# Chunk 0's triangular inverse: the step sizes move from its end into its start, and eight narrow products join TensorE's queue

## The chip, the cores and the metric

The kernel runs on one core of a Trainium2 chip. TensorE (PE) multiplies matrices, VectorE (DVE), ScalarE (ACT) and GpSimd (POOL) work on rows of SBUF and PSUM, and SyncE (SP) mostly issues DMAs. Each engine has a queue of its own and works through it in order; waits between engines are semaphores. The metric is the device time of one execution in microseconds; lower is better.

## The reference

The reference is a delta-rule attention followed by a feed-forward layer. For each of 4 x 8 heads, with 768 tokens of 48 values:

```python
k_n = k / (np.linalg.norm(k, axis=-1, keepdims=True) + 1e-06)
for t in range(S):
    y[:, :, t] = np.einsum('bhd,bhde->bhe', q[:, :, t], state)
    v_old = np.einsum('bhde,bhd->bhe', state, kt)
    state = state + bt[:, :, :, None] * np.einsum('bhd,bhe->bhde', kt, vt - v_old)
```

The heads' outputs, 3072 tokens of 384 values, then go through `h = x @ w_in`, `g = h * sigmoid(h)` and `g @ w_out` with 2048 inner values.

## The kernel before

**Chunks.** The 768 tokens of a head are cut into six chunks of 128. In a chunk the recurrence becomes a triangular system: with G the products of keys with keys, the kernel needs a matrix X that solves it, each row scaled by a step size that comes from beta and the key's length. The inverse is found on blocks of 32 tokens (T = 32), and four such blocks are then joined to 128 by small products on TensorE. Chunk 0 has a start of its own, because nothing else can be computed before it: there VectorE inverts halves of 16 (Q = 16), and TensorE joins 16 to 32, 32 to 64.

**The start, chunk 0, in order.**
- `square`, `add_squares`, `norm_steps`: lengths of the keys, by GpSimd and VectorE, and the step sizes, spread over the rows (`spread`).
- `turn(0, b, ...)` transposes keys and queries on TensorE (L500), `first_score` forms the products of keys with keys, and `block_out`/`block_in` bring their 32x32 blocks through DRAM to a layout in which each of 128 partitions holds one block: the tile g, in `sums_of_w` (L582). The tile x beside it is cleared by GpSimd (L564) and gets ones on its diagonal (L565), both in `block_room`.
- `block_steps(0)` gives `step`, 32 step sizes for each partition (product L445, copy by ScalarE L450).
- `first_queries(b)` forms keys times queries for the four batches (L529); ScalarE empties the banks (L544).
- `invert_first(step)` is the substitution on VectorE, on two 16x16 corners at a time. Before the change: g is multiplied by the steps (L668, step m on column m), then 15 rounds of a product (L676) and an addition (L680), and then x is multiplied by the steps, row by row (L683). Two block transposes follow (L690, L694).
- `joins(0)`: `corner` (TensorE L717, emptied by VectorE L724), `turned` (L733), `straight` (L746), `merge_half` (L806, twice without and twice with `second`). They end in xi, the inverse of 64 tokens, from which `solve(0)` goes on (L840, L884).

**Products nobody reads.** `busy(n)` puts n products of the identity with a zero state on TensorE (L347), each into the next of three banks (CC) and 384 columns wide unless `wide` says otherwise. In FP32 a product takes two passes, each a weight load and a matmul. Five of them stand between the last query score and the transposes of chunk 1's keys; each waits for one round of the substitution (after rounds 0, 1, 2, 4 and 8), a sixth for round 15.

**What sets the order.** The order is written out by hand: `pin` chains every instruction to the one before it on its engine, DMAs of SP are chained by `in_line`. Most weight and query loads are not placed by a stage but by a count: `begun` counts TensorE's instructions (4 for a product, 2 for a transpose), and each entry of `loads` is issued when the count reaches its number (L1344 to L1357), to wait for that product. The numbers are WINDOW + PACKET * k plus an offset, with PACKET = 256 and WINDOW = 445.

**The rest.** From about 60 us on TensorE works on the feed-forward of one chunk (`hidden` L1046, `project` L1090, `combine` L1163) while the scripts in `chunks` mix in the next chunk's attention.

Of the kernel before, what the change touches and what calls it, by code (L numbers as in the profile page):

```python
# [13 lines left out]
ALU = mybir.AluOpType  # L14
# [5 lines left out]
def kernel(  # L20
# [10 lines left out]
    nc = tc.nc  # L31
    B, H, S, D = q.shape
    DM, DFF = moe_w_in.shape
    P = 128
# [5 lines left out]
    W = 64  # L40
    T = 32
# [19 lines left out]
    def bank(room, name):  # L61

        tag = room[0]
        room.rotate(-1)
        return kept_banks.get(tag) or banks.tile([P, 512], FP32, name=name, tag=tag)
# [3 lines left out]
    def behind(later, earlier, how=NoSync):  # L69

        tc.add_manual_dep(
            later.ins, earlier.ins.name,
            mybir.DependencyInfo(how, mybir.DependencyReason.DATA), reason="order",
        )
# [3 lines left out]
    def pin(op):  # L78

        engine = op.ins.engine  # L80
        if engine in pins:
            behind(op, pins[engine])
        pins[engine] = op
        if engine in tensor[:1]:
            begun[0] += 2 if op.ins.is_transpose else 4
            while loads and begun[0] >= loads[0][0]:
                paced(*loads.popleft()[1:])
        return op
# [89 lines left out]
    def paced(fetch, *args):  # L178

        pace.append(pins[tensor[0]])  # L180
        fetch(*args)
# [32 lines left out]
    for e in range(2):  # L214
        for g in range(2):
            to, of = slice(HH * e + HH // 2 * g, HH * e + HH // 2 * (g + 1)), slice(HH // 2 * g, HH // 2 * (g + 1))
# [90 lines left out]
    def narrow_w_out(i):  # L307
# [14 lines left out]
        out=above[0:W], in_=above[0:W], pattern=[[1, W]], compare_op=ALU.is_gt, fill=0.0,  # L322
# [3 lines left out]
        out=above[W:P], in_=above[W:P], pattern=[[1, W]], compare_op=ALU.is_gt, fill=0.0,  # L326
# [16 lines left out]
    def busy(n=1, after=None, how=NoSync, wide=DM):  # L343

        for _ in range(n):
            pw = bank(CC, "pw")
            done = pin(nc.tensor.matmul(  # L347
                pw[:, 0:wide], lhsT=ident[:],
                rhs=states[0][:].rearrange("p u a w -> p (u a w)")[:, 0:wide], start=True, stop=True,
            ))  # L350
            tensor.append(done.ins.engine)
            if after is not None:
                behind(done, after, how)
                after = None
# [87 lines left out]
    def block_steps(c):  # L442

        pg = bank(A, "pg")
        pin(nc.tensor.matmul(  # L445
            pg[:, 0:T], lhsT=spread[:].rearrange("p j n -> p (j n)"), rhs=pick[:],
            start=True, stop=True,
        ))
        size = small.tile([P, T], FP32, name="step")
        pin(nc.scalar.copy(size[:], pg[:, 0:T]))  # L450
        return size
# [41 lines left out]
    def turn(c, b, j, room, by_vector=False):  # L493

        if j == 0:
            kq_room(c, b)
        src, kq = (kbufs[c % 2], queries[c] if c < 2 else None)[j][:, b], kqs[c, b]
        pt = bank(room, "pt")
        for p in range(NP):
            pin(nc.tensor.transpose(  # L500
                pt[:, p * C : (p + 1) * C], src[:, p].rearrange("p e w -> p (e w)"), ident[:]
            ))
        ptv = pt[:].rearrange("p (a t) -> p a t", a=NP)
        if j == 1:
            if by_vector:
                pin(nc.vector.tensor_scalar(
                    out=kq[:, :, j, :], in0=ptv, scalar1=-1.0, scalar2=None, op0=ALU.mult
                ))
            else:
                pin(nc.scalar.mul(kq[:, :, j, :], ptv, -1.0))  # L510
        elif by_vector:
            pin(nc.vector.tensor_copy(out=kq[:, :, j, :], in_=ptv))
        else:
            pin(nc.scalar.copy(kq[:, :, j, :], ptv))

    def score(c, b, js, rooms, evacuate):

        g, u = b // HB, b % HB
        if (c, g) not in aps:
            aps[c, g] = {}  # L520
        for j in js:
            if j not in aps[c, g]:
                aps[c, g][j] = work.tile([P, HB, H, W], FP32, name=f"ap{j}", tag=f"ap{j}", bufs=2)
        ap, kq, n = aps[c, g], kqs[c, b], len(js)
        pa = [bank(room, f"pa{e}") for e, room in enumerate(rooms)]
        for p in range(NP):
            for e, hf in ((0, 0), (1, 1), (0, 1), (1, 0)):
                rows, half = slice(W * e, W * e + D), slice(W * hf, W * (hf + 1))
                pin(nc.tensor.matmul(  # L529
                    pa[e][half, p * n * W : (p + 1) * n * W], lhsT=kq[rows, p, 0, half],  # L530
                    rhs=kq[rows, p, js[0] : js[-1] + 1, half], start=True, stop=True,
                ))
        for e in range(2):
            of = pa[e][:, 0 : NP * n * W].rearrange("p (a j t) -> p a j t", a=NP, j=n)
            for i, j in enumerate(js):
                evacuate(j, e, ap[j][:, u, e::2, :], of[:, :, i, :])
# [6 lines left out]
    def by_act(to, of):  # L543
        return pin(nc.scalar.copy(to, of))  # L544
# [7 lines left out]
    blocks = {}  # L552

    def block_room(c):

        if c == 0:
            g, x = (sum_room[:, at : at + T * T] for at in (AT_G, AT_X))
        else:
            g = work.tile([P, T * T], FP32, name="g", tag="g", bufs=1)[:]
            x = (  # L560
                sum_room[:, AT_LAST : AT_LAST + T * T] if c == 1
                else work.tile([P, T * T], FP32, name="x", tag="x", bufs=1)[:]
            )
        pin(nc.gpsimd.memset(x, 0.0))  # L564
        pin(nc.gpsimd.memset(x[:, 0 : T * T : T + 1], 1.0))  # L565
        g, x = (t.rearrange("p (s t) -> p s t", t=T) for t in (g, x))
        blocks[c] = (tc.dram_tile([P, T, T], FP32, name=f"blocks{c}"), g, x)

# [88 lines left out]
    Q, ys = T // 2, {}  # L657

    def corners(at):
        two = sum_room[:, at : at + 2 * Q * (T + 1)].rearrange("p (i r) -> p i r", i=2)  # L660
        return two[:, :, 0 : Q * T].rearrange("p i (s t) -> p i s t", t=T)[:, :, :, 0:Q]

    def invert_first(step):

        x = blocks.pop(0)[2]
        g2, x2 = corners(AT_G), corners(AT_X)
        of = step[:].rearrange("p (i m) -> p i m", i=2)
        yield pin(nc.vector.tensor_tensor(  # L668
            out=g2, in0=g2, in1=of.unsqueeze(2).to_broadcast([P, 2, Q, Q]), op=ALU.mult
        ))  # L670
        for m in range(Q - 1, 0, -1):
            n = Q - m
            t = work.tile([P, T * T // 4], FP32, name="rank1", bufs=1)
# [3 lines left out]
                out=tv, in0=g2[:, :, 0:m, m : m + 1].to_broadcast(shape),  # L677
                in1=x2[:, :, m : m + 1, m:Q].to_broadcast(shape), op=ALU.mult,
            ))
            yield pin(nc.vector.tensor_tensor(  # L680
                out=x2[:, :, 0:m, m:Q], in0=x2[:, :, 0:m, m:Q], in1=tv, op=ALU.add
            ))
        yield pin(nc.vector.tensor_tensor(  # L683
            out=x2, in0=x2, in1=of.unsqueeze(3).to_broadcast([P, 2, Q, Q]), op=ALU.mult
        ))
        rows = [slice(T * j, T * (j + 1)) for j in range(NB)]
        low = sum_room[:, AT_LOW : AT_LOW + BH * Q].rearrange("p (n s) -> p n s", s=Q)
        y = sum_room[:, AT_G : AT_G + BH * T].rearrange("p (n s) -> p n s", s=T)
# [3 lines left out]
            out=y[:, :, Q:T], in_=pick[:, Q:T].unsqueeze(1).to_broadcast([P, BH, Q])  # L692
        ))
        pin(nc.vector.transpose(  # L694
            out=up.rearrange("p n t -> p t n"), in_=x.rearrange("p s t -> p t s")
# [603 lines left out]
    for b in range(B):  # L1299
        square(0, b)  # L1300
    block_room(0)
    for b in range(2):
        turn(0, b, 0, M, b % 2 == 0)
# [10 lines left out]
    def first_queries(b):  # L1314

        def evacuate(j, e, to, of):
            by_act(to, of)

        score(0, b, (1,), (A, CC), evacuate)
# [8 lines left out]
    busy(3)  # L1328
    first_queries(1)
    step = block_steps(0)  # L1330
    for t in xis:
        pin(nc.gpsimd.memset(t, 0.0))
    paced(fetch_w_in, 0)
# [7 lines left out]
        turn(0, b, 1, M)  # L1341
    for b in range(2, B):
        first_queries(b)
    PACKET, WINDOW = 256, 445  # L1344
    loads.extend((
        (WINDOW + PACKET * 2 + 15, fetch_w_in, 2),
# [18 lines left out]
            out=to, in0=to, in1=above[:].unsqueeze(1).to_broadcast([P, H, W]), op=ALU.mult  # L1365
        ))

    for n in range(1 + Q):
        done = next(inv)
        if n in (0, 1, 2, 4, 8):  # L1370
            busy(1, done, Sync)
        if n == 10:
            turn(1, 0, 0, M)
        if n == 12:
            turn(1, 1, 0, M)
        if n == 14:
            turn(1, 2, 0, M)
        if n == 15:
            busy(1, done, Sync)
            turn(1, 3, 0, M)  # L1380
# [67 lines left out]
    def prepare(c):  # L1448
# [7 lines left out]
        def scored(b):  # L1456
            if b == 0:
                block_room(c)
            score(c, b, (0, 1), (A, CC), evacuate)
            if b % HB == 1:  # L1460
                block_out(c, b // HB)
# [114 lines left out]
    for c in range(1, NCH):  # L1576
# [5 lines left out]
        for word in chunks[c].split():  # L1582
            what, n = word[0], int(word[1:] or 1)
# [6 lines left out]
            elif what == "g":  # L1590
                step = block_steps(c + 1)
# [47 lines left out]
```

## Time and profile before

| what | value |
|---|---|
| time, median of 3 runs | 639.25 us (639.19 to 642.03) |
| span of the profiled execution | 636.1 us |
| TensorE busy | 622.4 us, 98% |
| VectorE busy | 397.5 us, 62% |
| ScalarE busy | 214.3 us, 34% |
| GpSimd busy | 89.9 us, 14% |
| mean granted TensorE clock | 0.986 |

The profiled execution's own time is not given beside its span; the median of the runs is 3.15 us above the span. In the profile's rows the first two numbers of a timeline or chain row are the start and the length in microseconds from the span's start; "x8" is a count; "[3.01 <-DMA ...]" is the idle time of the engine before the row and what ended it. "PEld" is the weight load that belongs to a matmul. "issue" in the chain is time in which the engine waited for nothing that the profile shows. A row of a stretch gives its length, then busy time and instruction count of PE, PEld, DVE, ACT and POOL, then the granted clock as a share of full, the busy share of the DMA engines and GB/s.

### The profile page before, as it was taken

How to read it: one execution, taken by the hardware profiler on the slowest of the kernel's cores; microseconds unless marked ns; L12 is line 12 of the kernel's file. 1: busy time of each engine (PE TensorE's matmuls, PEld its weight loads, DVE VectorE, ACT ScalarE, POOL GpSimd, SP SyncE). 2: the span in 40 equal slices, each digit the busy share in tenths (PEclk: the TensorE clock that was granted, in tenths of full speed). 3: DMA queues.
4: the chain of work that ended last, by engine and by line, in shares of the span. 5: the costliest groups of instructions: out<-in, count | busy, mean ns of one | idle time of the engine just before them, and what ended most of it. 6: DMA issues, size and time to landing. Idle time of an engine off the chain costs nothing.

```text
span 636.1 us, 21387 instructions
## 1 busy us (share of the span) xinstructions
PE 622.4 (98%) x9406; PEld 547.3 (86%) x9406; DVE 397.5 (62%) x910; ACT 214.3 (34%) x500; POOL 89.9 (14%) x92
## 2 busy tenths in 40 slices
PE   7979999999999999999999999999999999999997
PEld 5568788656799989989989989989989989989997
DVE  5786879999677974546974555975455964112112
ACT  3456673423351122451122451122451122441120
POOL 5033721345020020020020010020002000000000
PEclk9779999999999999999999999999999999999999
DMA  7966726350458460459151359232253133010101
GB/s 114 227 159 177 218 67 148 100 99 4 95 105 174 72 104 8 94 107 183 37 91 21 75 124 164 56 84 29 64 117 76 26 75 37 16 38 1 26 0 26
DMA packets 145676, 54.70 MB, mean 86 GB/s; under 512 B 117152, under 2 KB 138912, under 8 KB 145584
## 3 DMA queue, kind: packets, MB, share of 16 engines
q1 hardware_dynamic: 143136, 52.93, 40.5%
q8 instruction: 74, 1.21, 0.8%
q10 hardware_dynamic: 2448, 0.41, 0.4%
q14 instruction: 18, 0.15, 0.1%
HBM read 40.14 MB, written 11.01 MB: 80 GB/s over the span
## 4 chain that ended last, share of the span: by engine, by line
PE 94%; DVE 2%; DMA 1%; issue 1%; ACTq 0%; ACT 0%; POOL 0%; SPq 0%; DVEq 0%; POOLq 0%
PE phid L1046 40%; PE px L1163 17%; PE py L1163 13%; PE po L1090 5%; PE pb_c L840 3%; PE pa L529 2%; PE pb_c L828 2%; PE pyc L919 2%; PE pb_c L1090 2%; PE pb_c L860 2%; PE pyc L906 1%; PE px L782 1%; PE py L782 1%; PE pt L500 1%; DMA sums_of_w<-blocks 1%
## 5 line engine op out<-in xcount | busy, mean ns | idle before, releaser
L1046 PE MATMUL phid<-xT,w_in 128*128 128x256 f32 x1152 | 257.0, 381 | 0.2 <-DVE xT L893 0.2
L1046 PEld LDWEIGHTS phid<-xT,w_in 128*128 128x128 f32 x1152 | 216.4, 190 | 30.2 <-issue 0.9
L1056 ACT ACTIVATE gT<-phid 128x512 f32<-128x512 f32 x88 | 52.5, 597 | 144.8 <-PE phid L1046 140.5
L1144 DVE TENSOR_TENSOR sums_of_g<-gT 128x384 f32<-128x384 f32 (+1 forms) x60 | 30.4, 529 | 65.7 <-ACT gT L1056 55.4
L627 DVE SCALAR_TENSOR_TENSOR rank<-g,step,x 128x31 f32<-128x31 f32 (+15 forms) x124 | 49.8, 401 | 21.7 <-DMA g<-blocks 18.1
L1163 PE MATMUL px<-sums_of_w,sums_of_g 128*128 128x192 f32 x320 | 56.6, 329 | 0.0
L1163 PE MATMUL py<-w_out,sums_of_g 128*128 128x192 f32 x320 | 56.2, 328 | 0.0
L1163 PEld LDWEIGHTS py<-w_out,sums_of_g 128*128 128x128 f32 x320 | 52.3, 190 | 0.3
L1163 PEld LDWEIGHTS px<-sums_of_w,sums_of_g 128*128 128x128 f32 x320 | 52.2, 190 | 0.4
L632 DVE TENSOR_TENSOR x<-x,rank 128x31 f32<-128x31 f32 (+15 forms) x124 | 42.5, 342 | 4.3
L467 POOL TENSOR_TENSOR vf<-vf,n_slot 128x768 f32<-128x768 f32 x10 | 14.8, 1494 | 174.4 <-DMA vf<-in_v_dram 150.4
L544 ACT COPY xT<-pyc 48x128 f32<-48x128 f32 (+2 forms) x126 | 32.7, 260 | 1.7
L488 DVE STREAM_TRANSPOSE kq<-stage 128x512 f32<-128x512 f32 x28 | 28.4, 1115 | 5.2 <-DMA stage<-in_q_dram 5.2
L1163 PE MATMUL py<-w_out,gT 128*128 128x192 f32 x160 | 28.9, 330 | 0.0
L1174 DVE TENSOR_TENSOR o<-o,kept 128x192 f32<-128x192 f32 (+1 forms) x29 | 11.5, 422 | 26.7 <-ACT kept L1171 26.7
L1163 PE MATMUL px<-w_out,gT 128*128 128x192 f32 x160 | 27.9, 327 | 0.0
L1163 PE MATMUL px<-sums_of_w,gT 128*128 128x192 f32 x160 | 27.8, 327 | 0.0
L1163 PEld LDWEIGHTS px<-w_out,gT 128*128 128x128 f32 x160 | 26.5, 190 | 0.6
L550 POOL COPY g<-x 64x256 f32<-64x256 f32 x4 | 5.0, 1242 | 151.9 <-DVE x L635 151.9
L1163 PEld LDWEIGHTS py<-w_out,gT 128*128 128x128 f32 x160 | 26.1, 190 | 0.4
L865 DVE TENSOR_TENSOR state<-state,pb_c 128x384 f32<-128x384 f32 x22 | 11.2, 550 | 24.1 <-PE pb_c L860 24.1
L1163 PEld LDWEIGHTS px<-sums_of_w,gT 128*128 128x128 f32 x160 | 26.2, 190 | 0.1
(222 smaller groups left out, 931.2 us busy)
## 6 DMA issues: line engine op xcount, KB each, us to landing
vf<-in_v_dram SPq DMA_DIRECT2D x48, 96.0 KB, 2.8
out_dram<-o SPq DMA_DIRECT2D x42, 96.0 KB, 2.2
w_out<-in_moe_w_in_dram SPq DMA_DIRECT2D x4, 768.0 KB, 4.7
sums_of_w<-in_moe_w_out_dram SPq DMA_DIRECT2D x4, 768.0 KB, 4.1
blocks<-ap SPq DMA_DIRECT2D x44, 64.0 KB, 1.9
g<-blocks SPq DMA_DIRECT2D x5, 512.0 KB, 3.5
kb<-in_k_dram SPq DMA_DIRECT2D x12, 192.0 KB, 4.2
kb<-in_k_dram SPq DMA_DIRECT2D x24, 96.0 KB, 4.3
```

The source lines that it names most:

```text
L467: pin(nc.gpsimd.tensor_tensor(out=vf, in0=vf, in1=of, op=ALU.mult))
L488: pin(nc.vector.transpose(out=kqs[c, b][:, :, j, :].rearrange("p a (i m) -> p a m i", i=T), in_=src.rearrange("p a (m d) -> p a m d", d=D) ...
L529: pin(nc.tensor.matmul(pa[e][half, p * n * W : (p + 1) * n * W], lhsT=kq[rows, p, 0, half], rhs=kq[rows, p, js[0] : js[-1] + 1, half], sta ...
L544: return pin(nc.scalar.copy(to, of))
L627: pin(nc.vector.scalar_tensor_tensor(out=tv, in0=g[:, 0:m, m : m + 1].to_broadcast([P, m, n]), scalar=step[:, m : m + 1], in1=x[:, m : m + ...
L632: yield pin(nc.vector.tensor_tensor(out=x[:, 0:m, m:T], in0=x[:, 0:m, m:T], in1=tv, op=ALU.add))
L840: yield pin(nc.tensor.matmul(pz[rows, n * D : (n + 1) * D], lhsT=xis[g][rows, u * H + 2 * p + e, :], rhs=vfs[c][rows, hf, g * HB + u, p, : ...
L1046: pin(nc.tensor.matmul(ph[:, j * GT : (j + 1) * GT], lhsT=w_in[:, a, (2 * f + j) * P : (2 * f + j + 1) * P], rhs=xTs[c, hf][:, a, :], star ...
L1056: pin(nc.scalar.activation(out=hidden_of(c, hf, f), in_=ph[:], func=ACTF.Silu, scale=-0.5 if in_blocks(c) else 0.5))
L1090: pin(nc.tensor.matmul(pos[i][:, 0:DM], lhsT=hidden_of(0, hf, f // 2)[:, at : at + C], rhs=w_outs[f // HFF][:, f % HFF, :], start=(f == 0) ...
L1144: pin(nc.vector.tensor_tensor(out=sums_of_g[:, k, fs], in0=of[0], in1=of[1], op=op))
L1163: pin(nc.tensor.matmul(to, lhsT=at, rhs=quarter(f, *b) if isinstance(b, tuple) else sums_of_w[b][:, f], start=start and f == 0, stop=f == ...
```

## The change

Chunk 0's substitution gets its step sizes at the start. The diagonal of x holds the step sizes instead of ones: `block_room` leaves the memset of ones out for chunk 0, and a GpSimd copy from `step` writes the diagonal once `block_steps(0)` is done, ahead of the clearing of xi. g is multiplied with the step of its row instead of its column, that is with another axis of the step tile broadcast. The product of x with the steps at the end goes, and with it one step of the generator, so the loop that drives it runs Q times instead of 1 + Q.

Behind the last of chunk 0's query scores, ahead of the five wide products, stand eight products of 64 columns that nothing reads (`busy(8, wide=W)`, W = 64). They add 32 to the count that places the loads.

```diff
@@ block_room @@
         pin(nc.gpsimd.memset(x, 0.0))
-        pin(nc.gpsimd.memset(x[:, 0 : T * T : T + 1], 1.0))
+        if c > 0:
+            pin(nc.gpsimd.memset(x[:, 0 : T * T : T + 1], 1.0))
@@ invert_first @@
         yield pin(nc.vector.tensor_tensor(
-            out=g2, in0=g2, in1=of.unsqueeze(2).to_broadcast([P, 2, Q, Q]), op=ALU.mult
+            out=g2, in0=g2, in1=of.unsqueeze(3).to_broadcast([P, 2, Q, Q]), op=ALU.mult
         ))
...
-        yield pin(nc.vector.tensor_tensor(
-            out=x2, in0=x2, in1=of.unsqueeze(3).to_broadcast([P, 2, Q, Q]), op=ALU.mult
-        ))
         rows = [slice(T * j, T * (j + 1)) for j in range(NB)]
@@ the start of chunk 0 @@
     step = block_steps(0)
+    pin(nc.gpsimd.tensor_copy(
+        out=blocks[0][2].rearrange("p s t -> p (s t)")[:, 0 : T * T : T + 1], in_=step[:]
+    ))
     for t in xis:
         pin(nc.gpsimd.memset(t, 0.0))
...
     for b in range(2, B):
         first_queries(b)
+    busy(8, wide=W)
     PACKET, WINDOW = 256, 445
...
-    for n in range(1 + Q):
+    for n in range(Q):
         done = next(inv)
         if n in (0, 1, 2, 4, 8):
             busy(1, done, Sync)
```

## The prediction

> **What bounds the kernel now.** I read the page first (shares of the span, granted clock, queues), then busy time by stretch, then the chain of waits around the change.
>
> ```profile
> span 636.1 us, 21387 instructions
> PE 622.4 (98%) x9406; PEld 547.3 (86%) x9406; DVE 397.5 (62%) x910; ACT 214.3 (34%) x500; POOL 89.9 (14%) x92
> PEclk9779999999999999999999999999999999999999
> q8 instruction: 74, 1.21, 0.8%
> ```
> ```profile
> 100.00:150.00 50.00, 49.96 (x363) 33.93 (x361) 48.05 (x74) 17.55 (x25) 17.47 (x11) 1.00 0.44 102
> ```
>
> TensorE is busy 98% of the span, and in this 50 us stretch all of it. So a microsecond gained or lost in the first 50 us is carried to the end, because what follows is one TensorE queue without holes. The clock digits fall to 7 in the second and third slice only: there lie the change and the one stage in which TensorE waits. The 30 to 43 us part of the chain (start, length, what):
>
> ```profile
> 31.52 0.99 DVE sums_of_w L683
> 32.54 1.04 DVE sums_of_w L690
> 33.58 1.82 DVE sums_of_w L694
> ...
> 36.79 0.21 PE pb_c L733
> ...
> 38.09 1.05 issue
> 39.14 0.26 PE pb_c L806
> ...
> 41.62 1.35 issue
> ```
>
> VectorE leads until 36.8 us, the removed product (L683) among it. Then come two holes in which TensorE waited for no semaphore. By the count of instructions in program order, 256 TensorE instructions lie between them, and q8 brought 1.21 MB in 74 packets for 18,812 TensorE instructions, 254 to a packet: each hole is a packet of the instruction stream that was late. The clock, in stretches laid on its own edges (us, then busy time of TensorE, its weight loads, VectorE, ScalarE, GpSimd, then the clock):
>
> ```profile
> 17.97:21.38 3.41, 2.52 (x14) 1.72 (x15) 1.00 (x8) 1.46 (x8) 0.00 (x0) 1.00 0.90 246
> 21.38:24.79 3.41, 3.41 (x70) 2.79 (x69) 2.39 (x9) 2.39 (x7) 0.00 (x0) 0.50 1.16 266
> 24.79:28.21 3.42, 3.42 (x7) 1.77 (x6) 3.04 (x12) 1.77 (x3) 0.00 (x0) 0.50 1.16 151
> 35.03:38.45 3.42, 2.39 (x137) 1.99 (x132) 2.94 (x8) 1.25 (x4) 2.85 (x2) 1.00 0.47 89
> 38.45:41.86 3.41, 2.48 (x127) 2.35 (x128) 3.29 (x7) 1.60 (x6) 0.91 (x1) 0.50 0.64 215
> 41.86:45.27 3.41, 2.30 (x72) 2.24 (x73) 2.23 (x5) 2.78 (x5) 0.92 (x1) 0.50 0.79 254
> 45.27:48.69 3.42, 3.42 (x82) 3.42 (x82) 3.23 (x7) 0.48 (x2) 0.00 (x0) 0.50 0.47 87
> 48.69:52.10 3.41, 3.41 (x196) 3.09 (x189) 2.67 (x5) 2.74 (x6) 1.91 (x1) 1.00 0.58 113
> ```
>
> The clock is half from 21.4 to 28.2 and from 38.45 to 48.7, and it changes only on a grid of 3.41 us. A busy stretch does not lift it by itself (21.38 to 24.79 was full, and half stayed); long streaming does (24.79 to 28.21).
>
> **The change, part by part.** The rows that price it:
>
> ```profile
> 18.82 0.19 ACT L450 COPY step<-pg 128x32 f32<-128x32 f32 x1 [0.33 <-PE pg L445]
> 11.15 1.85 POOL L1332 MEMSET xi<- 128x1024 f32 x2
> 22.06 0.69 DVE L668 TENSOR_TENSOR sums_of_w<-sums_of_w,step 128x512 f32<-128x512 f32 x1 [3.01 <-DMA sums_of_w<-blocks]
> 22.85 0.21 DVE L676 TENSOR_TENSOR rank<-sums_of_w 128x30 f32<-128x30 f32 x1
> 31.33 0.63 POOL L691 COPY sums_of_w<-pick 128x512 f32<-128x512 f32 x1 [18.33 <-DVE rank L676]
> 18.38 0.30 PEld L445 LDWEIGHTS pg<-pick,spread 128*128 128x128 f32 x2 [0.72 <-issue]
> 24.51 0.38 ACT L544 COPY ap<-pb_c 128x256 f32<-128x256 f32 x1
> 24.12 5.50 PE L347 MATMUL pb_c<-state,ident 128*128 128x384 f32 x10
> 29.46 1.04 PE L500 MATMUL pt<-ident,kb 128*128 128x128 f32 x8
> 30.73 0.66 PE L500 MATMUL pt<-ident,kb 128*128 128x128 f32 x4 [0.24 <-ACT stage L514]
> 31.54 0.91 PE L347 MATMUL pb_c<-state,ident 128*128 128x384 f32 x2
> 32.29 0.60 PE L500 MATMUL pt<-ident,kb 128*128 128x128 f32 x4
> 33.63 0.20 PE L717 MATMUL pl<-sums_of_w,ap 32*32 32x16 f32 x2 [0.74 <-DVE sums_of_w L690]
> 44.83 1.88 PE pb_c L840 x32
> ```
>
> *The product at the end goes:* 31.52 to 32.54, 1.02 us off VectorE. *The product at the start* takes over its broadcast (step constant along the inner axis). That form took 0.99 us in L683, the old one 0.69 in L668: 0 to 0.30 us more. I take 0.30, the row with the same form, though L691 on GpSimd ran beside it and may be the cause. VectorE then gains 0.72 us (0.72 to 1.02), and L717 could start at 32.9 instead of 33.63.
>
> *The diagonal* was a memset behind L564; now a GpSimd copy waits for step (19.01 us), and behind it on GpSimd stand the two memsets of xi (1.85 us) and L691. An estimate from the memsets: under 0.3 us for the copy, so all is done by 21.2. The first reader of x is L676 at 22.85, held by the landing of the blocks; xi is written after 36.8, and L691 stands at 31.33. Cost nothing; should the blocks land 3.5 us earlier, the copy would be on the path at its full length.
>
> *Eight narrow products* stand on TensorE ahead of the five wide ones (24.12 to 29.46, each two passes, back to back; their waits for VectorE no longer bind). Each narrow one is two passes of a 128-column weight load and 64 columns. Two such loads with little to stream (L445) took 0.30 us, 0.19 each by their own length, so a pass per 0.11 us at full clock, 0.22 at half: 16 x 0.22 = 3.5 us. Bounds: by streaming alone, 64/384 of a wide pass (ten from 24.12 to 29.46, 4.1 us at half and 1.25 at full clock, so 0.66 us each at half and 0.33 at full), 1.8 us; load and stream one after the other, 5.2. I take 3.5: L445 has the same weights and few columns. The third narrow one also waits for the bank that ScalarE empties near 24.9; by then the first two have run 0.9 us, so nothing.
>
> What that delays is TensorE's own queue up to L717. Wide products would start at 27.6. **Half clock to 31.6 (case H):** by 31.62 they have done 4.0/0.66 = 6.1 of 10 passes, the rest takes 3.9 x 0.33 = 1.3, to 32.9. Then transposes, ScalarE copies, one wide product and transposes, by the rows 1.27 + 0.5 + 0.75 + 0.5 = 3.0: L717 starts at 35.9, 2.3 later than now. VectorE's gain is gone: L724 waits for TensorE, and its last ends near 38.2 (now just ahead of L733's 36.79).
>
> *The packet boundary* falls 30 instructions earlier in the work (32 added, two waiting ones fewer). Now the boundary before the first hole stands just behind L733's wait: crossed at about 36.05, packet there 39.14, 3.1 us later. In the changed order it lies in L717's products, about 1.0 us after their start, with no wait ahead: the next packet comes at 35.9 + 1.0 + 3.1 = 40.0 in H. The straight products reach the boundary at about 39.5 (1.3 us behind L724, as 36.79 to 38.09), so the hole shrinks to 0.5, and L806 starts at 40.1, 0.95 late. The second hole ends 3.83 us after the first (39.14 to 42.97), and 22 more instructions are left behind it (estimate 0.25): L840 starts at 40.0 + 3.83 + 0.25 + 1.86 = 45.94, where it now starts at 44.83, 1.86 behind the second hole. So 1.1 us late, at half clock until 48.7, worth 0.55 us of the work that follows.
>
> The Trainium skill (Runtime: NRT & Kernel Launch, Instruction fetch mechanics) says that crossing a 16 KiB block costs one tail bump, mostly hidden. This trace differs: 1.05 and 1.35 us of holes. By the page the two holes would be no term at all and this step would cost nothing.
>
> *Loads by count* (weights and queries) move with the boundary, 8 products earlier in the work; one piece of w_out goes ahead of chunk 1's values on SP's queue:
>
> ```profile
> 98.33 5.65 SPq L198 DMA_DIRECT2D vf<-in_v_dram  x8
> 129.82 3.09 POOL L467 TENSOR_TENSOR vf<-vf,n_slot 128x768 f32<-128x768 f32 x2
> ```
> ```profile
> PE pyc L919 <- issue: 0.8, 1, 0.8
> ```
>
> They land some 25 us before L467 reads them; one more issue ahead is hidden. Later boundaries shift too; the hole of 0.8 us before L919 (at 87 us) goes and one like it comes 3 us sooner: 0, plus or minus 0.8.
>
> **Sum for H:** -0.72 on VectorE, not reached; +1.1 at L840; 0.55 at the end. The profiled span is 636.1, 3.15 below the median; I leave that distance as it is and count from 639.25: 639.8 us.
>
> **Rivals.** *F, the clock lifts at 28.2 as now.* The narrow passes stream half of their time, so 24.79 to 28.21 would stream about 60% where the wide ones fill it. For it: weight loads leave no idle time. Against it: the full stretch 21.38 to 24.79 did not lift it. Then the wide products end at 27.6 + 0.6 + 9.1 x 0.33 = 31.2, L717 starts at 34.2, the packet comes at 38.3, L840 starts at 44.25: 0.6 early, 0.3 at the end: 638.95. The Trainium skill (TensorE: Matmul & The Clock Gate, Part 1) gives full rate after one busy window of about 3.4 us, free-running; by that rule F holds. The trace has the grid, but the busy stretch at 21.38 speaks against reading "busy" so simply.
>
> *S, slower: half clock outlasts 48.7.* L840 starts later, and 45.27 to 48.69 (full now) holds more of the thin 32x32 products, which did not lift it at 41.86 or 45.27. One window more at half costs 3.41/2 = 1.7: 641.5; two, 643.2. It decides if L840 begins after about 46.5. For it: H is only 0.55 short of that. Against: L840 and L884 stay dense.
>
> *E, faster: half clock ends at 45.27,* since in F denser work moves ahead: 638.95 - 1.7 = 637.25; if it never falls at 38.45, 42.97 to 48.69 runs at full, -2.9: 636.0. Against both: 2.3 to 2.5 of 3.41 us busy there now, and 0.6 us moves little.
>
> **Chances and range.** 0.5% (3.2 us) is about what a measurement of this kernel can tell from no change. H 0.42 (639.8), F 0.30 (638.95), S 0.09 (641.5) and 0.08 (643.2), E 0.07 (637.25) and 0.04 (636.0). So faster 0.04, same 0.88, slower 0.08. I forecast H. The range 637.2 to 641.7 leaves out the outermost S and E, 0.12; H's own: with 1.8 for the narrow products L717 starts at 35.0, with 5.2 at 36.8, 0.9 to either side and 0.45 at the end; with 0.8 for the later holes, 638.5 to 641.1.
>
> **What would show it.** VectorE: no L683 form behind L680, the first product 0.7 to 1.0. TensorE: narrow products from 24.1 for 3.5 us, wide ones later, and no hole between the straight products and L806, or one of half a microsecond before their end. Clock: the edge at 28.2 or 31.6 parts F from H; the edges at 38.45 and 48.7 part S and E. Wrong would be: narrow products near 1.8 us with the clock lifted at 28.2 (then L717 starts by 33.2 and VectorE's gain arrives), or a clock edge elsewhere, which outweighs every other term.

## The result and the profile after

The changed kernel takes 645.3 us (median of 16 runs, 641.57 to 647.89), the kernel before 639.85 us (16 runs, 637.8 to 642.03). The ratio is 1.0075, with a 95% interval of 1.0058 to 1.0093. The change costs some 5 us. The forecast was 639.8 us and no change, and its range ended at 641.7: it was wrong.

The page of the changed kernel, the lines that answer to those of before:

```profile
span 644.4 us, 21418 instructions
...
PE 624.3 (97%) x9422; PEld 549.5 (85%) x9422; DVE 395.4 (61%) x909; ACT 214.1 (33%) x500; POOL 90.1 (14%) x92
...
PEclk9968999999999999999999999999999999999999
...
q8 instruction: 74, 1.21, 0.8%
```

TensorE is busy 1.9 us longer, but the span is 8.3 us longer. So most of the loss is time in which TensorE stands still. The profiled execution of before was one of its fastest: in the runs the time is 1.7 us above the span, so its 636.1 us stand for 637.8, the lowest of its 16. (The profiled one of after took 646.11, which is near its median.) A fairer base is the new substitution without the narrow products, the first experiment below, whose profiled execution lies at its median: span 638.6, TensorE busy 621.8. Against it 2.5 of 5.8 us are busy time and 3.3 are idle.

What TensorE waited for in the changed kernel (in all, times, longest, in us; from the substitution on, line numbers are two smaller than before):

```profile
PE pl L715 <- issue: 2.1, 1, 2.1
PE pb_c L838 <- issue: 2.1, 2, 1.1
PE px L1161 <- issue: 1.8, 2, 1.5
PE phid L1044 <- DMA xT<-part: 1.6, 1, 1.6
PE py L804 <- issue: 1.3, 1, 1.3
PE pt L500 <- DMA kb<-in_k_dram: 1.1, 1, 1.1
...
PE pb_c L744 <- issue: 0.9, 1, 0.9
...
PE pyc L917 <- issue: 0.6, 1, 0.6
```

Before, holes of this kind ("issue") came to 2.4 us at L806, 0.8 at L919 and 0.5 at L733. Now they are 2.1, 2.1, 1.8, 1.3, 0.9 and 0.6. Two waits for DMAs have grown: the one for `xT` is new, and the one for `kb` is 1.7 us with the new substitution alone too, which costs nothing (below). The chain of the changed kernel through the stage of the change (start, length, what):

```profile
32.45 0.13 PE pl L715 x2
...
33.70 2.11 issue
35.81 0.24 PE pl L715 x4
...
38.78 0.85 issue
...
41.89 1.30 issue
...
45.31 1.15 issue
46.46 0.63 PE pb_c L838 x6
```

The corner's products (L715) begin at 32.38 us, 1.25 earlier than before (33.63). VectorE's gain had arrived. Then TensorE stands still for 2.11 us in the middle of them, at 33.70, with all their inputs there. Three more holes follow, where before there were two. The first L838 starts at 46.46 us, where L840 of before started at 44.76.

Which of these holes are late packets of instructions can be counted. In program order (two instructions for each matmul record, and the waits in the weight-load queue), the holes of 2.11, 0.85 and 1.30 us, and three later ones of 0.92, 0.58 and 1.49 us, end at instructions 960, 1217, 1472, 3776, 4033 and 13760. These are multiples of 256 apart, to one instruction. The hole of 1.15 us before the first L838 ends at instruction 1627, so it is no packet's end (nor is the 0.5 us at L733 before, which ends at 955). At the first L838 ScalarE is late with its copies of `xi`, behind its work on the weights (L233, L234):

```profile
45.00 0.97 ACT L234 ACTIVATE w_out<-w_out,plus 128x768 int32<-128x768 uint32 x1
46.00 0.63 ACT L544 COPY xi<-px 32x256 f32<-32x256 f32 x2
```

Before, ScalarE did these two pieces of work while TensorE stood in the hole of 1.35 us, and copied `xi` at 43.97. In the changed kernel that hole ends ahead of the products that ScalarE must copy first, so its work on the weights starts only behind the hole (44.19). The hole of 1.0 to 1.2 us before the first L838, and ScalarE's order, are the same in every run below that moves the packets by a part of one, and in no other. So it follows from the place of the packets, but at one remove.

### The profile page after: what moved, and what is told of

It is laid out like the page before. It is cut to its first block, busy times and chain, and to the rows that moved or that the text cites. A ratio compares the mean times of both kernels' runs of the same rounds, so it can differ in the third digit from the quotient of the medians.

```text
span 644.4 us, 21418 instructions
## 1 busy us (share of the span) xinstructions
PE 624.3 (97%) x9422; PEld 549.5 (85%) x9422; DVE 395.4 (61%) x909; ACT 214.1 (33%) x500; POOL 90.1 (14%) x92
## 4 chain that ended last, share of the span: by engine, by line
PE 93%; issue 2%; SPq 1%; DVE 1%; DMA 1%; ACT 1%; POOL 0%; DVEq 0%; POOLq 0%
PE phid L1044 39%; PE px L1161 17%; PE py L1161 12%; PE po L1088 5%; PE pb_c L838 3%; PE pa L529 2%; PE pb_c L826 2%; PE pyc L917 2%; PE pb_c L1088 2%; PE pb_c L858 1%; PE pt L500 1%; PE pyc L904 1%; SPq L144 1%; PE px L780 1%; PE py L780 1%
## 5 line engine op out<-in xcount | busy, mean ns | idle before, releaser
L1161 PE MATMUL px<-sums_of_w,sums_of_g 128*128 128x192 f32 x320 | 56.9, 329 | 0.3 <-issue 0.3
L1161 PE MATMUL py<-w_out,sums_of_g 128*128 128x192 f32 x320 | 56.2, 328 | 0.0
L1161 PEld LDWEIGHTS px<-sums_of_w,sums_of_g 128*128 128x128 f32 x320 | 52.2, 190 | 1.0 <-issue 0.6
L1161 PEld LDWEIGHTS py<-w_out,sums_of_g 128*128 128x128 f32 x320 | 52.3, 190 | 0.3
L1161 PE MATMUL px<-sums_of_w,gT 128*128 128x192 f32 x160 | 28.0, 327 | 1.5 <-issue 1.5
L1161 PE MATMUL py<-w_out,gT 128*128 128x192 f32 x160 | 28.9, 330 | 0.0
L1172 DVE TENSOR_TENSOR o<-o,kept 128x192 f32<-128x192 f32 (+1 forms) x29 | 11.5, 423 | 26.9 <-ACT kept L1169 26.9
L1161 PE MATMUL px<-w_out,gT 128*128 128x192 f32 x160 | 27.9, 327 | 0.0
L1161 PEld LDWEIGHTS px<-sums_of_w,gT 128*128 128x128 f32 x160 | 26.2, 190 | 1.7 <-issue 1.6
L838 PE MATMUL pb_c<-vf,xi 64*64 64x48 f32 x736 | 25.2, 223 | 2.1 <-issue 2.1
L838 PEld LDWEIGHTS pb_c<-vf,xi 64*64 64x64 f32 x736 | 23.5, 138 | 4.3 <-issue 3.6
L1161 PEld LDWEIGHTS px<-w_out,gT 128*128 128x128 f32 x160 | 26.5, 190 | 0.6
L1161 PEld LDWEIGHTS py<-w_out,gT 128*128 128x128 f32 x160 | 26.1, 190 | 0.4
```

Source lines behind the costliest of these rows:

```text
L838: yield pin(nc.tensor.matmul(pz[rows, n * D : (n + 1) * D], lhsT=xis[g][rows, u * H + 2 * p + e, :], rhs=vfs[c][rows, hf, g * HB + u, p, : ...
L1161: pin(nc.tensor.matmul(to, lhsT=at, rhs=quarter(f, *b) if isinstance(b, tuple) else sums_of_w[b][:, f], start=start and f == 0, stop=f == ...
```

## What the experiments had to tell apart

Five theories (the last formed after the first eight runs), by the letters that the expectations use. P: it matters where the packets of TensorE's instruction stream end. The 8 narrow products put 32 instructions in front of everything that follows, two waiting ones of L347 go with them (the traces of before and of the substitution alone have these two, those with the narrow products don't), and a packet holds 256. V: the new substitution costs the time. T: the narrow products cost it by the time that TensorE spends on them. L: the loads that are issued by count come at another time. N: each instruction that is added in front costs something, wherever packets end.

### One part alone

**The substitution without the narrow products.**

```diff
-    busy(8, wide=W)
```

> The new substitution alone, without the eight narrow products: TensorE's queue has the instructions of before at the same places. Theory P (packets): the loss comes from the instruction stream, whose packet boundaries fall 30 instructions earlier in the work, so that a packet is needed inside L717's products before it has come; without the narrow products no loss is left and VectorE's 0.7 to 1.0 us arrive at least in part: 638.8 to 639.9 against 639.85. Theory V (the substitution itself costs, by its new broadcast or the copy on GpSimd): 641 or more. Theory T (TensorE's time for the narrow products): as P, 638.8 to 639.9.

Measured: 640.46 us against 640.87 of before, ratio 0.9992 (0.9981 to 1.0003). V is out: the new substitution costs nothing. Nor is a gain shown, since the interval holds 1. The corner's products start at 32.48 us, 1.15 earlier than before, and this is taken back behind them. The chain of this kernel:

```profile
34.88 0.96 issue
35.84 0.25 PE pb_c L731
...
38.55 1.02 issue
...
42.05 1.36 issue
```

The last two holes are those of before (1.05 and 1.35). The first is new: TensorE is ready sooner, and the packet is not.

**The narrow products with the old substitution.**

```diff
     for b in range(2, B):
         first_queries(b)
+    busy(8, wide=W)
```

> The eight narrow products alone, with the old substitution. P and T: the loss stays, 644 to 646.5. V: near before, 639 to 640.5.

Measured: 647.03 us, ratio 1.0094 (1.0073 to 1.0115). The narrow products alone cost as much as the whole change, and the changed kernel's hole before the combine and its wait for the transposed copies are there again:

```profile
PE px L1163 <- issue: 2.2, 2, 1.5
PE pb_c L840 <- issue: 1.8, 2, 1.1
PE py L806 <- issue: 1.6, 1, 1.6
PE phid L1046 <- DMA xT<-part: 1.6, 1, 1.6
```

### Their instructions, or their time

**The narrow products at the kernel's start.**

```diff
-    busy(3)
+    busy(2)
+    busy(9, wide=W)
...
-    busy(8, wide=W)
```

> All of the change, but the narrow products stand at the very start of the kernel, in place of one wide product (nine narrow for one wide and eight), where TensorE waits for the first keys: the instructions behind are shifted by 32, without the narrow products' time at 24 us. P: the loss stays at least in half, 642.5 to 646. T: the loss goes, 638.8 to 640. Loads keep their place against the packets as in the changed kernel, so a cost of the earlier loads (theory L) would stay too.

Measured: 650.49 us, ratio 1.0148 (1.0127 to 1.0169). This one does not decide between P and T: the narrow products delayed the first transposes (8.85 instead of 6.39 us), the clock rose only at 11.5 us, and half clock lasted from 32.0 to 55.9. It does show 0.213 us for each narrow pass at half clock.

**The loads back at their old places.**

```diff
-    PACKET, WINDOW = 256, 445
+    PACKET, WINDOW = 256, 477
```

> The changed kernel with 32 added to the count at which the loads are issued: every load is again behind the same product as before, and SP's queue has its old order; packets and narrow products stay as in the changed kernel. P and T: the loss stays, 643.5 to 646.5. L (loads 8 products earlier in the work, a piece of w_out ahead of chunk 1's values): back to 639 to 641.

Measured: 646.16 us, ratio 1.008 (1.0064 to 1.0097), with holes at the same instructions as in the changed kernel. L is out.

**Eight tiny products for the eight narrow ones.** The helper, which the next one uses too:

```diff
+    def tiny(n):
+        for _ in range(n):
+            pw = bank(CC, "pw")
+            done = pin(nc.tensor.matmul(
+                pw[0:32, 0:16], lhsT=ident[0:32, 0:32],
+                rhs=states[0][:].rearrange("p u a w -> p (u a w)")[0:32, 0:16], start=True, stop=True,
+            ))
+            tensor.append(done.ins.engine)
...
-    busy(8, wide=W)
+    tiny(8)
```

> The changed kernel with its 8 narrow products (128x128 weights, 64 columns) replaced by 8 tiny ones (32x32 weights, 16 columns) at the same place: the same 32 instructions in TensorE's stream, about a tenth of the time on TensorE. Theory P (what costs is where the packets of TensorE's instruction stream end): nothing of the loss goes, 644 to 647 us, with the hole of about 2 us among L715's products (here 11 lines lower, L726). Theory T (what costs is the time that the narrow products take on TensorE, 2.3 us): the loss goes, 640 to 641 us.

Measured: 646.33 us, ratio 1.008 (1.0065 to 1.0095). T is out: the 16 tiny passes took 0.9 us of TensorE at half clock, where 16 narrow ones take 3.4 (0.213 each), and the loss is all there. The hole inside the corner's products, which P expected, did not show. In this execution half clock lay from 21.1 to 31.4 us, so the corner started 2.2 us later than with the substitution alone, and its packet was there by then. The later holes came (1.6 before L755, 1.0 at L815, 2.1 at L849).

**More time on TensorE without more instructions.** The substitution alone, with the five wide products at 512 columns:

```diff
         if n in (0, 1, 2, 4, 8):
-            busy(1, done, Sync)
+            busy(1, done, Sync, 512)
```

> The new substitution alone, without the narrow products, but the five wide unread products with 512 columns in place of 384: no instruction more, 1.1 us more on TensorE at full clock, 2.1 at half. Theory P: 640 to 641.5 us, holes as in the substitution alone. Theory T: half of the loss of the narrow ones, 643 us or more.

Measured: 640.81 us, ratio 0.9993 (0.9977 to 1.0009). Time that lies beside VectorE's substitution is free, as T denies.

### Other lengths in front

**56 tiny products behind the narrow ones.** The changed kernel with

```diff
     busy(8, wide=W)
-    PACKET, WINDOW = 256, 445
+    tiny(56)
+    PACKET, WINDOW = 256, 701
```

> The changed kernel with 56 tiny products (32x32, 16 columns) behind its 8 narrow ones, and the loads' count moved with them: 254 instructions more than the substitution alone, one whole packet less 2, so every later packet ends where it ended before the change. TensorE has about 2 us more to do than in the changed kernel. Theory P: the loss goes in spite of that, 640 to 642 us (up to 0.8 us of the 2 us reach the path behind the wait for chunk 1's keys), no hole among the corner's products, holes before the turned and the straight products as before the change. Theory T: the loss grows, 646 to 649 us.

Measured: 646.2 us, ratio 1.0082 (1.0049 to 1.0114): the time that T expected. The trace shows one reason. Its execution was the slowest of the six (650.06; the others go down to 642.54), and in it the clock was half from 21.6 to 38.6 us. The narrow products took 3.6 us (24.20 to 27.80) and the 56 tiny ones, all on one quarter of TensorE, 6.1 instead of 2, far more than VectorE's work covers. The corner's products started 10.0 us later than with the substitution alone, and the last product of the kernel 9.7 later. Nothing was lost behind the start, but that had to be shown with a cheaper filling (below).

**Fourteen narrow products.**

```diff
-    busy(8, wide=W)
+    busy(14, wide=W)
```

> The changed kernel with 14 narrow products in place of 8: 24 instructions and 1.7 us of TensorE more. The packet end that the changed kernel meets behind the wait for chunk 1's keys is met ahead of it. Theory P: the hole among the corner's products (2.1 us) goes, and the time is 0.5 to 4 us under the changed kernel's, as far as the later holes stay; theory T: it is slower by 1 us or more, 646 us and up.

Measured: 649.01 us, ratio 1.0137 (1.0115 to 1.0158). The hole inside the corner's products went, as P said, but the gain that P expected did not come: the later holes grew (3.1 us before L804, 2.0 before L826), and one more stretch of half clock came at 440.7 us. The number was T's, for another reason, as the 13 tiny ones below show.

**64 tiny products spread over the four quarters, nothing else.** The substitution alone, with this helper in place of the one above:

```diff
+    def tiny(n):
+        for i in range(n):
+            of = slice(32 * (i % 4), 32 * (i % 4) + 32)
+            pw = bank(CC, "pw")
+            done = pin(nc.tensor.matmul(
+                pw[of, 0:16], lhsT=ident[of, of],
+                rhs=states[0][:].rearrange("p u a w -> p (u a w)")[of, 0:16],
+                start=True, stop=True, tile_position=(of.start, of.start),
+            ))
+            tensor.append(done.ins.engine)
...
-    PACKET, WINDOW = 256, 445
+    tiny(64)
+    PACKET, WINDOW = 256, 701
```

> The new substitution without the narrow products, with 64 tiny products in their place (32x32 weights, 16 columns, on the four diagonal quarters of TensorE in turn, some 1.5 to 3 us in all), the loads' count moved with them: 256 instructions, so every later packet ends where it ends with the substitution alone. Theory P (where packets end decides): 640 to 642 us, no loss behind the first 60 us. Rival N (every instruction added in front costs, wherever packets end): eight times the instructions of the narrow ones, 650 us or more.

Measured: 641.99 us, ratio 1.0017 (1.0006 to 1.0028).

**The changed kernel with 56 of them.** As above, with

```diff
+    busy(8, wide=W)
+    tiny(56)
+    PACKET, WINDOW = 256, 701
```

> The changed kernel with 56 such tiny products behind its 8 narrow ones, loads' count moved: again 256 instructions in all, and the narrow products are done. P: 640.5 to 643 us, the loss of the change goes although TensorE does more than in the changed kernel; the holes of 2.1 us among the corner's products, of 1.5 us before L1161 (here 12 lines lower) and the wait of 1.6 us for the transposed copies go. N: 650 us or more.

Measured: 642.26 us, ratio 1.0027 (1.0004 to 1.0051).

**Half a packet.** The same helper, with

```diff
-    PACKET, WINDOW = 256, 445
+    tiny(32)
+    PACKET, WINDOW = 256, 573
```

> The new substitution with 32 tiny products (128 instructions, half a packet), loads' count moved. P: every packet ends half a packet earlier in the work, so the time differs from the substitution alone by the holes at other places, 638 to 650 us, and the holes of the substitution alone before the turned and the straight products are not at the same instructions. N: 646 to 650 us, half of what 64 cost, with the holes in place.

Measured: 652.54 us, ratio 1.0172 (1.0154 to 1.0191).

**A fifth of a packet.** The same helper, with

```diff
-    PACKET, WINDOW = 256, 445
+    tiny(13)
+    PACKET, WINDOW = 256, 497
```

> The new substitution with 13 tiny products (52 instructions), loads' count moved: the packet end that the changed kernel meets behind the wait for chunk 1's keys is met ahead of it, as with 14 narrow ones. P: no hole among the corner's products, holes at the same instructions as with 14 narrow ones and about their loss, 646 to 650 us. N: between the substitution alone and 32 tiny ones, 641 to 645 us.

Measured: 649.13 us, ratio 1.0117 (1.0099 to 1.0134).

N is out: 13, 32 and 64 tiny products give 649.1, 652.5 and 642.0 us. A whole packet more costs 1.5 us against the substitution alone, a part of one costs 9 to 12. Half a packet cost even more than P's 650. The unread products also turn the rotation of the three banks, but this is not the cause: 13 and 64 turn it by the same one step, and differ by 7 us. And 56 tiny products put behind the changed kernel's narrow ones make it faster, by some 3 us. The busy times on the page of the one with half a packet, and on that of the one with narrow and tiny products (those of the changed kernel stand above):

```profile
span 650.2 us, 21513 instructions
...
PE 624.3 (96%) x9470; PEld 547.7 (84%) x9470; DVE 397.8 (61%) x909; ACT 214.1 (33%) x500; POOL 90.3 (14%) x92
```
```profile
span 639.9 us, 21641 instructions
...
PE 624.0 (98%) x9534; PEld 548.6 (86%) x9534; DVE 396.3 (62%) x909; ACT 214.2 (33%) x500; POOL 90.0 (14%) x92
```

In these three TensorE's busy time is the same to 0.3 us (624.3, 624.3, 624.0), with spans of 644.4, 650.2 and 639.9. What differs is where it stands still. The waits of TensorE in the kernel with narrow and tiny products (line numbers 12 larger than in the changed kernel):

```profile
PE py L816 <- issue: 2.0, 1, 2.0
PE pyc L929 <- issue: 1.6, 2, 1.3
PE pb_c L816 <- issue: 1.4, 1, 1.4
...
PE pl L743 <- issue: 0.8, 1, 0.8
```

No hole among the corner's products (L727), none before the combine (L1173), no wait for the transposed copies. Where in the kernel each one loses, instruction by instruction against the substitution alone (us later than there):

| kernel | first of corner | first L838 | 58 us | chunk 0's hidden, 95 us | L1161, 434 us | last product |
|---|---|---|---|---|---|---|
| changed | -0.1 | +1.3 | +2.8 | +5.7 | +7.0 | +5.7 |
| narrow alone | +0.9 | +0.2 | +0.4 | +2.5 | +5.4 | +3.8 |
| 13 tiny | +0.3 | +0.6 | +1.8 | +4.2 | +9.0 | +8.7 |
| 32 tiny | -0.4 | +0.6 | +5.5 | +6.0 | +11.0 | +11.5 |
| 64 tiny | +0.3 | -0.6 | +0.6 | +1.3 | +1.5 | +1.7 |
| narrow and 56 tiny | +1.8 | +1.0 | +1.1 | +1.8 | +1.2 | +1.3 |

In the four that move the packets by a part of one, the loss grows in the same stretches, up to 400 us behind the edit. Behind the first L838 it grows by 3.6 to 10.9 us. In the two that move them by a whole one it grows by 2.3 and 0.3. Each row is one execution: that of before, laid beside the substitution alone in the same way, gains 2.1 us behind the first L838, so a difference of 2 us in this table tells little. Of the four only the changed kernel stands still for more than 0.3 us inside these first corner's products. So the loss does not hang on that hole, but on the later ones.

## Why the prediction was wrong, point by point

**VectorE: the mechanism was right, one term mis-sized.** The product at the end is gone. The one at the start has the new broadcast and takes no longer than the old one:

```profile
21.62 0.69 DVE L669 TENSOR_TENSOR sums_of_w<-sums_of_w,step 128x512 f32<-128x512 f32 x1 [2.44 <-DMA sums_of_w<-blocks]
...
31.08 1.07 DVE L688 STREAM_TRANSPOSE sums_of_w<-sums_of_w 128x512 f32<-128x512 f32 x1
```

From first product to transpose it is 9.46 us, before 10.48 (22.06 to 32.54): 1.02 gained, where I took 0.72. The 0.30 that I added for the broadcast was nothing.

**The diagonal: right.** GpSimd's copy took 0.24 us at 19.28 ("under 0.3"), the memsets of xi end at 21.26, and the first product waits for the DMA of the blocks as before. (All rows of GpSimd in these two traces name SBUF tiles; PSUM banks are emptied by VectorE and ScalarE.)

**The narrow products: right in what bounds them, wrong in what they delay.** All 16 passes, stretch 22.7 to 25.1 us, ran from 22.80 to 25.07:

```profile
L347 PE MATMUL pb_c<-state,ident 128*128 128x64 f32 x16 | 2.3, 284 | 0.1
```

That is 0.14 us for a pass at full clock, where 0.11 was worked out, and 0.213 at half clock at the kernel's start, where 0.22 was. But the clock was full here until 35.9, and the corner's products started at 32.38, neither at 35.9 (H) nor at 34.2 (F). Whether the clock drops near 21 us differs between the profiled executions: it did before the change and with 8 or 64 tiny products, and did not in the changed kernel and with the substitution alone. I took one execution's clock for the kernel's own.

**The packet boundary: the step that failed.** The prediction took what follows the first 50 us for "one TensorE queue without holes". Of the boundaries it followed one, the one behind L733's wait, put it into L717's products "with no wait ahead", and let the first hole shrink to 0.5 us. It did shrink, from 1.05 to 0.85 (38.78 above). But the same shift puts the boundary of the packet before it to another place too, and this was not looked at: the packet that begins near the end of the corner's products is now needed 30 instructions sooner, inside them. When it can come is shown by the instruction transfers and by the waits for chunk 1's keys. The changed kernel, the waits in the weight-load queue, and then the instruction queue in the stretch 32.9 to 33.2 us (packets, MB, share):

```profile
L500 PEldq EVENT_SEMAPHORE  x4: 51/51/51, 27.1 to 30.4; - x4
```
```profile
q8 instruction: 1, 0.02, 27.5%
```

The last wait for the keys (`PE pt L500 <- DMA kb<-in_k_dram`) passes at 30.4, the transfer starts at 33.04, and the hole ends at 35.81. By the order of instructions, the end of the packet before it stands at just those waiting instructions. With 14 narrow products it stands a few instructions ahead of the first of them, and the transfer starts at 26.59, before the waits pass (27.0 to 30.1). This fits a request that is made when the queue gets past the end of the packet before, and that a semaphore wait there holds up. It is not shown: with 13 tiny ones the end stands ahead of the first wait too, four instructions further on in the work, and that wait passes at 27.5; yet the transfer starts at 31.39, behind the last wait (30.72). A rival stays open. From 30 to 33 us other loads fill the DMA engines (shares of 1.03, 1.16 and 1.41 of all 16 in the changed kernel, 0.87 from 33 on), and the packet's transfer may have stood behind them. Before the change this packet was as late (its transfer starts at 32.47), but it was needed only behind L733's wait for VectorE, at about 36.05, and so it cost nothing.

The Trainium skill (Runtime: NRT & Kernel Launch, Instruction fetch mechanics) says that the next page is fetched while the current one runs. The traces agree: the transfers at 33.04, 36.95 and 40.74 us each start while the packet before runs. It also says that the cost of crossing from one to the next is mostly hidden. This case does not agree, where a page runs faster than the next one comes: in the changed kernel the transfers at 33.04, 36.95 and 40.74 end holes at 35.81, 39.64 and 43.19, so 2.5 to 2.8 us from start to use. Where small products are dense, more than a page runs in that time. The chain at 436 us, in the changed kernel and, at the same instructions, before:

```profile
436.59 1.22 PE py L780 x82
437.81 1.08 PE pb_c L826 x64
438.89 0.52 PE px L1161 x2
439.41 1.49 issue
440.90 2.44 PE px L1161 x14
```
```profile
430.26 1.22 PE py L782 x82
431.48 1.08 PE pb_c L828 x64
432.56 2.80 PE px L1163 x16
```

Here 146 small matmuls, each with its weight load, run in 2.3 us, and the packet behind them is late. Before, the same packet began 15 matmuls later, behind wide ones that take 2.8 us, and no hole shows.

**Later boundaries, "0, plus or minus 0.8": wrong by several us.** I had one hole before L919 swap with one like it. What came is the 1.49 above, a hole of 0.9 before L838 at 86.7 us, and 0.58 before L917. The last two add to what makes ScalarE late, and this makes a wait of a kind that I had not priced: chunk 0's transposed copies come too late for the second half of the hidden layer. The chain of the changed kernel:

```profile
86.65 0.92 issue
...
91.09 0.58 issue
...
95.02 0.71 SPq L897
...
97.74 3.34 DMA xT<-part
...
101.22 2.83 PE phid L1044 x12
```

SP's queue before the change:

```profile
89.78 3.32 SPq L899 DMA_DIRECT2D xT<-part  x5
```

SP issued the copies from 89.78 us on, and now does so from 95.02, 5.24 later. TensorE did not wait for them before (the first hidden layer went on to 92.5, from 88.44), and now waits 1.6 us.

**Half clock: rival S, with a chance of 0.17, came true in this execution.** "It decides if L840 begins after about 46.5": L838 began at 46.46. That H had 45.94 for this start, only 0.5 us off, is luck: the corner's products began 3.5 us earlier than in H, and two holes that H did not have (2.11 and 1.15) took it back. The stretches of the clock's grid in the changed kernel (length, busy times, then the granted clock):

```profile
42.74:46.16 3.42, 2.12 (x77) 1.98 (x76) 2.83 (x7) 2.31 (x4) 1.27 (x1) 0.50 0.95 281
46.16:49.57 3.41, 3.11 (x58) 3.15 (x59) 2.62 (x5) 0.94 (x3) 0.00 (x0) 0.50 0.28 47
49.57:52.98 3.41, 3.41 (x66) 3.29 (x65) 2.55 (x5) 1.35 (x3) 1.10 (x1) 0.50 0.56 103
52.98:56.40 3.42, 3.27 (x159) 2.83 (x159) 1.66 (x4) 2.99 (x5) 0.81 (x1) 1.00 0.33 50
```

By itself S would have given 641.5 to 643.2, so it is a part of the loss. The dense work missed the edge at 46.16 by 0.3 us, and the clock rose one stretch later, after the first that was busy throughout; before, this was 45.27 to 48.69. The Trainium skill (TensorE: Matmul & The Clock Gate, Part 1) has full rate after one busy window, and these two edges agree; the stretch of before from 21.38 to 24.79, which was busy throughout, does not. Half clock went on until 52.98, one stretch longer than with the substitution alone (35.68 to 49.33), but the grid lies elsewhere in each execution (edges 0.89 us apart in these two), so that part of the loss is not a constant: the kernel with 64 tiny products had half clock to 51.4 and still took 642 us.

**The loads moved: right**, nothing, by the fourth run. **The base: wrong.** I took 3.15 us for the usual distance of time and span. It is 1.7, so the profiled execution was a fast one, and its clock and holes need not be the typical ones. The median itself moved by 0.6 with more runs.

**Sum.** H had +0.55 us. Of the measured 5, the runs give about -0.4 to the substitution (not told from 0), 6.2 to the narrow products alone, and 1.4 to them when 56 tiny ones fill up the packet, TensorE's time for all of these included: by far the most goes with the place of the packets, in idle time and in the clock that follows it. The term that was most mis-sized is "0, plus or minus 0.8" for the later boundaries: in the profiled executions the changed kernel is 1.3 us behind the substitution alone at the first L838, and 4.4 more are lost behind it. What stays open: what sets the time at which a packet's transfer starts, and how much of the loss is idle time by itself and how much is the clock that follows it, because the clock's grid can't be set. (With 14 narrow products, with 13 tiny ones and with the narrow ones at the kernel's start, the clock also fell to half at 440.7, 441.4 and 445.0 us.) Nor was a version found that is faster than the kernel before: the substitution alone is equal to it. Its 1.15 us at the corner would have to be kept from the packet behind, and no run here did that without losing more later.

## What to carry to other kernels

Where an engine runs hundreds of small instructions in a few microseconds, its instruction stream is a resource like any other: before adding "free" instructions, count them, and find every later place where a packet of 256 ends, not just the next one. A shift by a whole packet tells in one run whether a change costs by what it does or by where it moves the rest. And an engine's gain ahead of a stage is worth only what the next late thing leaves of it, which here was a packet of instructions that came later than the work.

## What the runs showed that was not expected

- The place of packets is worth up to 12 us of 640 in this kernel (640.5 us with the substitution alone, 652.5 with 128 instructions more that take 1.6 us), and half of that falls due 60 to 400 us behind the place of the edit.
- The same packet's transfer started at 26.59 us with 14 narrow products and at 31.39 with 13 tiny ones, four instructions fewer. Whether a semaphore wait or the busy DMA engines held it up is open.
- A late packet also moves work on another engine: ScalarE's 1.9 us on the weights, hidden in a hole of TensorE before, cost TensorE 1.15 us once the hole lay ahead of that work.
- A product with 128x128 weights in FP32 takes 0.28 us at full clock for 64 columns (2.27 us for 8), and 0.66 for 384: a sixth of the columns saves little more than half of the time.
- 56 tiny 32x32 products took 1.2 us when they went round the four quarters of TensorE at full clock (25.26 to 26.42), and 6.1 us on one quarter at half clock.
